# Key-value products three heads a matmul, a two-column tile of ones, and a last tile stored in three parts

## The chip, the cores and the metric

The kernel runs on one core of a Trainium2 chip. Its time is the device time of one execution in microseconds (us), and the median over several executions is quoted. The profile's span is about 1.4 us shorter than the time of the same execution. The three sets of experiments ran on three different chips, so each is compared in time with runs of the kernel before on its own chip; the kernel before has one profile only, from the start.

## The reference

Two linear-attention blocks A and B (sequence S = 2048, width D = 640, 32 heads of 20) read the same x; a sigmoid gate mixes their outputs. Shortened:

```python
def _A_ref(x, wqkv, wo):                      # _B_ref is the same
    q, k, v = split(x @ wqkv)                 # heads of 20
    phi = lambda t: jnp.where(t > 0, t + 1, jnp.exp(t)) + 1e-6
    pq, pk = phi(q), phi(k)
    kv  = einsum("bhsd,bhse->bhde", pk, v)    # 20 x 20 a head
    z   = einsum("bhsd->bhd", pk)
    num = einsum("bhqd,bhde->bhqe", pq, kv)
    den = einsum("bhqd,bhd->bhq", pq, z)[..., None] + 1e-6
    return (num / den).reshape(B, S, D) @ wo

g = sigmoid((x * gate_w).sum(-1, keepdims=True))
return g * a + (1 - g) * b
```

## The kernel before

The kernel first computes, for each branch, a Gram product of `pk` with x (lines L643 and L644, "Gram units" below), transposes it into `GS`, and multiplies that by the value weights `WV` to get the key-value products. This multiplication is the "burst" of L705. Six heads share a stationary tile of 128 columns, so a product holds blocks that belong to no head; the vector engine (DVE) multiplies by a 0/1 mask while it copies the product out of PSUM into `KVL`.

```python
KVL = {X: sb("KVL" + X, [128, NU, GR], bf) for X in XS}      # NU = 6, GR = 120
ONE = sb("ONE", [128, 128], bf)
...
for us in ((0, 1, 2, 3), (4, 5)):
    ps = Buf("kv", "ps")                    # one PSUM bank, from a pool of 8
    def fn(e, us=us, ps=ps):
        for i, u in enumerate(us):
            for c in range(NC):             # NC = 5
                lo, n, w = (GR * u, 128, 24) if u < 5 else (540, 104, 8)
                r = e.matmul(PS[0:n, ps.slot, GR * i : GR * i + NC * w],
                             WV[X][:, c, lo : lo + n], gv[:, c, :, 24 * u : 24 * u + w],
                             start=(c == 0), stop=(c == NC - 1))
    ...
    out(lambda ps=ps, n=n: PS[:, ps.slot, 0 : GR * n], us[0], n, 24, BDM, 0, 128)        # mask on DVE
    if 5 in us:
        out(lambda ps=ps: PS[64:104, ps.slot, GR : GR + 40], 5, 1, 8, BDE, 64, 104)
...
LAST = ((0, 512, "ACT"), (512, D, "DVE"))   # who copies which columns of the last output tile
def last_b(t):
    for (lo, hi, eng), ps in zip(LAST, blast):
        if hi == D:
            o_mm("A", t, ps, lo, hi)
        o_mm("B", t, ps, lo, hi)
        o_post(t, ps, lo, hi, eng, "ACT" if hi == D else "SP")   # copy, and store on this queue
```

A scheduler of the kernel's own puts the operations of each engine in order and gives out the PSUM banks when the program is built.

## Time and profile before

The median is 187.78 us (187.69 to 188.05, three runs); the profile has a span of 186.7 us. PE, the matrix engine, is the bound, so I cut the span where PE passes fixed points of the program. Each stage runs from the start of one matmul to that of another, in us:

| stage | before |
|---|---|
| start to first Gram matmul | 48.50 |
| first Gram matmul to first matmul of burst A | 52.07 |
| burst A to burst B | 41.63 |
| burst B to the last matmul | 42.15 |
| last matmul to the end of the span (the tail) | 2.32 |

The first stage contains the time at half clock, the last one the last copy and stores. "PE's stream" below is the sum of the three stages between them, 135.84 us here. The views print a span to 0.1 us; the tails in this document are taken to its unrounded end in the trace (186.669 us here). The expectations were written with rounded spans, so they name a tail of 2.36 us for 2.32. The prediction shows the engine totals, burst A and the tail. First, the timeline of PE after burst A and its query group: the Gram unit, whose first matmul starts at 103.18, and then the next query group. The first column is the start, the second how long the group is busy.

```profile
103.18 0.38 PE L643 MATMUL ps<-XN,PKB 128*128 128x512 bf16 x1
...
104.21 0.22 PE L644 MATMUL ps<-XN,PKB 128*128 128x129 bf16 x1
104.27 0.59 PE L797 MATMUL ps<-XT,WQB 128*128 128x512 bf16 x2
```

From 103.18 to 104.27 is 1.09 us, which is four pairs of 216 + 56 ns: PE doesn't wait. Second, the stores of the output by queue, with the shortest, median and longest duration in ns of the issuing instruction:

```profile
L354 SPq DMA_DIRECT2D out_dram<-TSB x16: 332/332/359, 164.8 to 184.7; - x16
L354 ACTq DMA_DIRECT2D out_dram<-TSB x1: 350/350/350, 185.0 to 185.0; - x1
```

Sixteen stores are issued on the queue of SP (an engine that issues transfers here), the last small one on that of the scalar engine (ACT), each in about a third of a microsecond.

### The profile page before, as it was taken

Reading aid. Unit: us, or ns where it says so; the run is one execution under the profiler, and the core shown is the slowest. Engines: PE = TensorE matmul, PEld = TensorE weight load, DVE = VectorE, ACT = ScalarE, POOL = GpSimd, SP = SyncE. Lnnn points to the kernel's source line nnn. Section 1 sums busy time; section 2 is a strip of 40 time slices with the busy share of each in tenths; the row PEclk is TensorE's granted clock in tenths of the full one; section 3 lists DMA queues with packets and bytes.
Section 4 is the critical chain, followed back from the end, with each engine's and each line's share of the span. In section 5 each row is a group of like instructions: output and inputs, shape, how many; then the busy total and the mean of one; then the engine's idle time right before and its main releaser. Section 6 shows DMA issues by size and latency. Waiting matters only on the chain.

```text
span 186.7 us, 3247 instructions
## 1 busy us (share of the span) xinstructions
PE 182.6 (98%) x1272; PEld 107.1 (57%) x1297; DVE 137.2 (73%) x264; ACT 95.0 (51%) x167; POOL 0.8 (0%) x10
## 2 busy tenths in 40 slices
PE   8999999999999999999999999999999999999995
PEld 4555555555555656555557555555567555555553
DVE  2289888888834455487799999998899999059563
ACT  5265655656454645544675666888623784400001
POOL 1000000000000000000000000000000000000000
PEclk9999999999999999999999999999999999999999
DMA  7989999995001011010511412126515447513424
GB/s 209 284 152 145 271 385 365 342 204 125 4 0 35 0 39 35 0 35 5 91 27 35 83 29 40 28 43 171 177 35 115 65 103 166 171 70 109 142 106 140
DMA packets 36501, 21.38 MB, mean 115 GB/s; under 512 B 25694, under 2 KB 36230, under 8 KB 36486
## 3 DMA queue, kind: packets, MB, share of 16 engines
q1 hardware_dynamic: 36044, 20.96, 44.7%
q10 hardware_dynamic: 442, 0.21, 0.4%
q8 instruction: 10, 0.16, 0.4%
q14 instruction: 5, 0.04, 0.1%
HBM read 10.87 MB, written 4.26 MB: 81 GB/s over the span
## 4 chain that ended last, share of the span: by engine, by line
PE 97%; DMA 1%; issue 1%; DVE 0%; DVEq 0%
PE ps L957 23%; PE ps L797 23%; PE ps L535 18%; PE ps L643 18%; PE ps L536 5%; PE ps L644 5%; PE ps L705 2%; DMA XN<-in_A_x_dram 1%; PE ps L740 1%; PE ps L479 1%; DVE TSB L1001 0%; PE ps L466 0%; DVEq L237 0%; PE ps L516 0%
## 5 line engine op out<-in xcount | busy, mean ns | idle before, releaser
L535 PE MATMUL ps<-WKW,XT 128*128 128x512 bf16 x154 | 43.8, 386 | 0.0
L814 ACT ACTIVATE EK<-ps 128x512 bf16<-128x512 f32 x40 | 23.9, 598 | 30.2 <-PE ps L797 27.9
L536 PE MATMUL ps<-WKW,XT 128*128 128x128 bf16 (+1 forms) x160 | 35.5, 222 | 0.3
L568 ACT ACTIVATE EK<-ps 128x640 bf16<-128x640 f32 x32 | 22.3, 704 | 10.7 <-DVE EK L571 5.3
L535 PEld LDWEIGHTS ps<-WKW,XT 128*128 128x128 bf16 x160 | 15.9, 99 | 19.1 <-issue 0.6
L797 PE MATMUL ps<-XT,WQA 128*128 128x512 bf16 x96 | 24.0, 379 | 0.1
L797 PE MATMUL ps<-XT,WQB 128*128 128x512 bf16 x96 | 23.6, 380 | 0.2
L643 PE MATMUL ps<-XN,PKA 128*128 128x512 bf16 x78 | 23.1, 379 | 0.1
L643 PE MATMUL ps<-XN,PKB 128*128 128x512 bf16 x78 | 23.1, 379 | 0.0
L824 DVE TENSOR_SCALAR EK<-EK 128x512 bf16<-128x512 bf16 x40 | 11.5, 289 | 13.5 <-ACT EK L814 13.5
L644 PE MATMUL ps<-XN,PKA 128*128 128x129 bf16 x80 | 17.6, 220 | 0.1
L644 PE MATMUL ps<-XN,PKB 128*128 128x129 bf16 x80 | 17.6, 220 | 0.1
L957 PE MATMUL ps<-WPA,EX 128*128 128x512 bf16 (+1 forms) x117 | 16.6, 297 | 0.2
L957 PE MATMUL ps<-WPB,PKA 128*128 128x512 bf16 (+1 forms) x118 | 16.4, 298 | 0.1
L536 PEld LDWEIGHTS ps<-WKW,XT 128*128 128x128 bf16 x160 | 15.9, 99 | 0.0
L797 PEld LDWEIGHTS ps<-XT,WQB 128*128 128x128 bf16 x100 | 10.9, 118 | 8.6 <-issue 0.4
L571 DVE TENSOR_SCALAR EK<-EK 128x640 bf16<-128x640 bf16 x32 | 10.4, 326 | 6.9 <-ACT EK L568 6.7
L797 PEld LDWEIGHTS ps<-XT,WQA 128*128 128x128 bf16 x100 | 10.7, 117 | 8.1
L643 PEld LDWEIGHTS ps<-XN,PKA 128*128 128x128 bf16 x80 | 9.4, 117 | 7.9
L643 PEld LDWEIGHTS ps<-XN,PKB 128*128 128x128 bf16 x80 | 9.4, 117 | 7.9
L579 DVE SCALAR_TENSOR_TENSOR PKA<-ps,EK 128x640 bf16<-128x640 f32 x16 | 13.2, 825 | 0.5
L579 DVE SCALAR_TENSOR_TENSOR PKB<-ps,EK 128x640 bf16<-128x640 f32 x16 | 13.2, 825 | 0.6
(77 smaller groups left out, 222.5 us busy)
## 6 DMA issues: line engine op xcount, KB each, us to landing
out_dram<-TSB SPq DMA_DIRECT2D x15, 160.0 KB, 1.8
XN<-in_A_x_dram SPq DMA_DIRECT2D x1, 2240.0 KB, 9.0
WKW<-in_A_wqkv_dram SPq DMA_DIRECT2D x5, 160.0 KB, 3.7
WKW<-in_B_wqkv_dram SPq DMA_DIRECT2D x5, 160.0 KB, 4.1
WQA<-in_A_wqkv_dram SPq DMA_DIRECT2D x1, 800.0 KB, 10.6
WQB<-in_B_wqkv_dram SPq DMA_DIRECT2D x1, 800.0 KB, 11.8
WVA<-in_A_wqkv_dram SPq DMA_DIRECT2D x1, 800.0 KB, 12.6
WVB<-in_B_wqkv_dram SPq DMA_DIRECT2D x1, 800.0 KB, 14.4
```

The lines of the kernel that those rows point to most:

```text
L535: e.matmul(a[:, 0:512], l, WK[X][:, c, 0:512], start=(c == 0), stop=(c == NC - 1))
L536: return e.matmul(a[:, 512:w], l, WK[X][:, c, 512:w], start=(c == 0), stop=(c == NC - 1))
L568: op("ACT", lambda e: e.activation(EK[:, ek.slot, :], psw(ps, D), ACT.Exp), act_cost(D), ins=[ps] + first, outs=[ek], name="ke")
L571: lambda e: e.tensor_scalar(EK[:, ek.slot, :], EK[:, ek.slot, :], 1.0, EPS, op0=ALU.min, op1=ALU.add),
L579: lambda e: e.scalar_tensor_tensor(PKt[X][:, t, :], psw(ps, D), 0.0, EK[:, ek.slot, :], op0=ALU.max, op1=ALU.add),
L643: e.matmul(a[:, 0:512], l, XN[:, t, 0:512], start=(t == 0), stop=(t == NT - 1))
L644: return e.matmul(a[:, 512 : D + 1], l, XN[:, t, 512 : D + 1], start=(t == 0), stop=(t == NT - 1))
L705: r = e.matmul(PS[0:n, ps.slot, GR * i : GR * i + NC * w], WV[X][:, c, lo : lo + n], gv[:, c, :, 24 * u : 24 * u + w], start=(c == 0), sto ...
L797: r = e.matmul(PS[:, ps.slot, :], WQ[X][:, c, g::5], XT[:, c, 512 * b : 512 * b + 512], start=(c == 0), stop=(c == NC - 1),)
L814: lambda e: e.activation(EQ[:, eq.slot, :], PS[:, ps.slot, :], ACT.Exp),
L824: lambda e: e.tensor_scalar(EQ[:, eq.slot, :], EQ[:, eq.slot, :], 1.0, EPS, op0=ALU.min, op1=ALU.add),
L957: r = e.matmul(a[:, l0 - lo : h0 - lo], PQ[X, b][:, g, 128 * (t % 4) : 128 * (t % 4) + 128], WP[X][:, g, l0:h0], start=(X == first and g = ...
```

## The change

No intent comes with it. What can be read off is that it saves SBUF, the memory beside the engines: 2 x 6 x 60 columns of `KVL`, 126 of `ONE` and 12 of the masks, 2 bytes each, are 1,716 bytes in each partition. Three things change, and they can be taken apart: the key-value part, the tile of ones, and the split end.

```diff
-    q, m = p % 64, np.arange(24)[None, :]
-    bd = np.where(p < 64, (q >= 4) & ((q - 4) // 20 == m // 4), (q < 60) & (3 + q // 20 == m // 4))
+    q, m = p % 64, np.arange(12)[None, :]
+    bd = np.where(p < 64, (q >= 4) & ((q - 4) // 20 == m // 4), (q < 60) & (q // 20 == m // 4))
...
-    KVL = {X: sb("KVL" + X, [128, NU, GR], bf) for X in XS}
+    KVL = {X: sb("KVL" + X, [128, NU, HR], bf) for X in XS}        # HR = 60
...
-    ONE = sb("ONE", [128, 128], bf)
+    ONE = sb("ONE", [128, 2], bf)              # its readers take ONE[:, 0:1] broadcast
...
-        for us in ((0, 1, 2, 3), (4, 5)):
+        for ts in (range(8), range(8, 11)):
...
-                        lo, n, w = (GR * u, 128, 24) if u < 5 else (540, 104, 8)
+                        lo, n, w = (GR * (t // 2), 128, 12) if t < 10 else (540, 104, 8)
                         r = e.matmul(
-                            PS[0:n, ps.slot, GR * i : GR * i + NC * w],
+                            PS[0:n, ps.slot, HR * i : HR * i + NC * w],
                             WV[X][:, c, lo : lo + n],
-                            gv[:, c, :, 24 * u : 24 * u + w],
+                            gv[:, c, :, 12 * t : 12 * t + w],
...
-            out(lambda ps=ps, n=n: PS[:, ps.slot, 0 : GR * n], us[0], n, 24, BDM, 0, 128)
+            for r in range(2):                 # upper and lower 64 partitions
+                out(lambda ps=ps, n=n, r=r: PS[64 * r : 64 * r + 64, ps.slot, 0 : GR * n]...[:, :, r, :],
+                    ts[0] // 2, n, 12, BDM[64 * r : 64 * r + 64, :], 64 * r, 64 * r + 64)
...
-    LAST = ((0, 512, "ACT"), (512, D, "DVE"))
+    LAST = ((0, 512, "ACT"), (512, 576, "DVE"), (576, D, "DVE"))
...
-            if hi == D:
+            if lo:
                 o_mm("A", t, ps, lo, hi)
             o_mm("B", t, ps, lo, hi)
-            o_post(t, ps, lo, hi, eng, "ACT" if hi == D else "SP")
+            o_post(t, ps, lo, hi, eng, "SP" if lo else "ACT")
```

## The prediction

> **What bounds the kernel now.** I read the page first, for the engine totals and the chain that ended last.
>
> ```profile
> PE 182.6 (98%) x1272; PEld 107.1 (57%) x1297; DVE 137.2 (73%) x264; ACT 95.0 (51%) x167; POOL 0.8 (0%) x10
> PE 97%; DMA 1%; issue 1%; DVE 0%; DVEq 0%
> ```
>
> The matrix engine PE is busy for 98% of the span of 186.7 us, and 97% of the chain of waits is PE itself. In the list of who waited for whom, PE's waits are 0.4 us for the tile of ones at the start and 0.2 us for the first input tile. Nothing holds it in the middle: where two matmul starts stand further apart than the matmul before them is wide, the excess is just one missing record (for instance 272 ns where 216 + 56 belong), apart from some 0.2 us at each of the four bursts that use 64-row tiles. So the time is a short head, one unbroken PE stream, and a tail after the last matmul. A change to the vector engine (DVE) or to buffers counts only if it makes PE wait.
>
> Next the timeline, for the stretches that the change touches. The first is the key-value burst of branch A on PE, then the weight loads (PEld) of the same line by form, then what DVE does with its result.
>
> ```profile
> 100.57 1.69 PE L705 MATMUL ps<-GSA,WVA 128*128 128x120 bf16 x30
> 102.11 0.81 PE L797 MATMUL ps<-XT,WQB 128*128 128x512 bf16 x3
> ...
> L705 PEld LDWEIGHTS ps<-GSA,WVA 128*128 128x128 bf16 x25 | 1.4, 98 | 0.2
> L705 PEld LDWEIGHTS ps<-GSA,WVA 128*104 128x104 bf16 x5 | 0.3, 128 | 0.0
> ...
> 101.90 2.13 DVE L685 TENSOR_TENSOR KVLA<-ps,CST 128x480 bf16<-128x480 f32 x3
> ```
>
> The burst costs PE 102.11 - 100.57 = 1.54 us from its first start to the next line's first start. The tail:
>
> ```profile
> 183.84 0.44 PE L957 MATMUL ps<-WPA,PKA 128*128 128x128 bf16 x5
> 184.10 0.60 ACT L1003 ACTIVATE TSB<-ps 128x512 bf16<-128x512 f32 x1 [21.89 <-PE ps L957]
> 184.12 0.44 PE L957 MATMUL ps<-WPB,GSA 128*128 128x128 bf16 x5
> 184.67 0.29 DVE L1001 CAST TSB<-ps 128x128 bf16<-128x128 f32 x1 [0.81 <-PE ps L957]
> 185.00 0.35 ACTq L354 DMA_DIRECT2D out_dram<-TSB  x1
> ```
>
> Ten matmuls of 128 columns, a copy of 0.29 us, an issue at 185.00 and a landing about 1.6 us after it (page, DMA issues) make the end at 186.7.
>
> **The price of one matmul in this trace.** Five matmuls of 128 columns take 184.12 - 183.84 = 0.28 us from start to start, 56 ns each. The chain has 30 matmuls of the output projection, 15 of 512 and 15 of 128 columns, in 4.08 us: 272 ns a pair, so 216 ns for 512 columns. The line through both is 0.417 ns a column plus 2.7 ns. It gives 52.7 ns at 120 columns; 25 of them are 1.32 us of the burst's 1.54, which leaves 0.22 us, 44 ns each, for the five matmuls of 40 columns, where the line would say 19 ns. Those five are the ones whose stationary tile has 104 columns: their loads last 128 ns and not 98. There the weight load, not the streaming, sets the pace.
>
> **What the Trainium skill says.** "TensorE: Matmul & The Clock Gate", section "Back-to-back issue gap", gives N/2.4 + 2.5 ns for a warm matmul; the line above agrees within 0.2 ns. The same section names a floor of about 25 ns for any N up to 64, and also about 62 ns a matmul where the sequencer decodes in software; the trace before has no long run of narrow matmuls, so it doesn't tell which floor this program has. The section "Weight-path perf modes — Fast Weight Load (FWL) and DoubleRow" says that a fast load is used when the stationary tile has 128 weights and isn't fp32; the 98 against 128 ns agree. "What's actually happening" in the same page puts the full clock after some 3.4 us of sustained activity; the trace has the full pace from 6.05 us, and PE busy without a gap from 2.7 us, which is 3.4 us earlier. "DMA: Bandwidth & Descriptors", section "Anatomy of one DMA — SWDGE (gpsimd) path", explains most of a DMA's fixed time as the write receipt; the three last stores here, of 160, 128 and 32 KB, land in 1.8, 1.7 and 1.6 us, so size hardly matters.
>
> **The change, part by part.** The build order of the changed kernel shows the same order on PE, with the burst split and the end split; ACT, POOL and SP keep theirs but for the last stores. DVE's order moves by a place here and there.
>
> (1) Key-value burst: per branch 25 matmuls of 120 columns become 50 of 60, and the five of 40 stay. The streamed columns are the same, 3,000; the fixed 2.7 ns and the weight load are paid twice. By the line 60 columns take 27.7 ns. The stationary tile keeps 128 columns, so the fast load should hide: five loads of 104 columns took 44 ns each, and a fast load must be well under that. Then a burst is 50 x 27.7 + 5 x 44 = 1.61 us against 1.54, +0.07 us, and +0.13 us for both branches. If a load and a matmul need some 30 ns together, it is 1.72 us, +0.36 us for both. I take +0.2 us. All of this is on the path, because PE never waits.
>
> (2) The masking on DVE: two operations of 64 partitions x 240 elements replace one of 128 x 480, and two of 64 x 60 one of 128 x 120. Elements along the free dimension are the same in sum, so the cost is two more instructions; DVE time goes by elements per partition, and the halves lie one after the other. The operation of 480 took 1.50 us and that of 40 took 0.275 us, which is 2.8 ns an element plus some 0.16 us. So 2 x 0.83 + 2 x 0.33 + 0.28 = 2.6 us against the 2.13 us in sequence: about +0.4 us per branch. None of it is on the path if it fits: for branch B the last masking ends at 145.57 us and PE's first user, the burst of L740, starts at 146.54, so about 0.9 us are spare. For branch A the user starts at 116.3, over 12 us later. DVE's later chain for branch B (scaling, first done at 154.9) has 7 us until PE needs it at about 162.
>
> (3) Ones as two columns: the fill on DVE took 0.17 us and will take perhaps 0.1 us less, so the first warming matmuls start at about 0.3 and not 0.39 us. They end before the first input tile lands at 2.6 us in either case, so nothing that counts moves. The full clock comes 3.4 us after PE's gapless activity starts at the landing of x, which is unchanged.
>
> (4) Last columns in two parts: 20 matmuls of 64 columns at 29.4 ns are 0.59 us against 10 x 56 = 0.56, +0.03 us. The last copy has 64 and not 128 columns, at about 1 ns a column -0.07 us. But both 64-column stores go to the SP queue, where an issue takes 0.33 us: first part copied at about 184.63, issued 184.66 to 184.99; second part copied at about 184.92 but issued at 184.99, when the queue is free. That is where the issue stood before, 185.00. Landing 1.6 us later: the gain is 0.0 to 0.05 us. The 512-column store moves to the ACT queue behind its own copy, at about 184.73, as before.
>
> Sum: +0.2 (1) + 0 (2) + 0 (3) + 0.0 (4) = +0.2 us, so 187.78 + 0.2 = 187.98; I say 187.95.
>
> **The rivals.** First: PE can't feed instructions fast enough. The burst becomes 110 instructions, a load and a matmul each 27.7 ns. For it speaks the software-decode figure above; against it that the L705 burst before ran 60 instructions at its streaming pace[...]. If it came, at 62 ns a matmul throughout, a burst would be 55 x 62 = 3.4 us, +1.9 us per branch and +3.7 us in all, 191.5 us, the one way to a loss of 2%. I give it 3%. Second: the masking of 64-partition operations costs more than its elements, say per row of the pattern, 1.5 us for each 240-element operation. It would be over 3 us, eat the 0.9 us of slack in branch B, and PE would wait some 0.5 us: 188.5 us. That the 40-element operation with short rows fits the price per element speaks against it. Third: the warm-up, started earlier, opens the full clock earlier. PE ran at half pace from 3.7 to 6.05 us; each us of that gone saves 0.5 us, so at most about -1 us, 187.0. The gap before the landing of x stays, which speaks against it. Fourth: the split tail gains its full 0.07 us or more; then the total is 187.9.
>
> **Range and chances.** Runs of the kernel before spread over 0.36 us. The sure terms run from +0.05 to +0.5 us; a drift between chips and a clock that opens slightly earlier pull below, a stretched burst above. I take 187.4 to 188.6. Within 2% means 184.0 to 191.5 us, and only the first rival reaches its edge; nothing I see reaches a gain of 3.8 us.
>
> **What would show each step.** For (1): the L705 burst of about 1.6 to 1.7 us from first start to the next line's, with matmul starts 27 to 30 ns apart; over 2 us says that the load or the feeding binds. For (2): the masking in about 2.6 us, and no wait of PE at the L740 burst of branch B. For (3): the first full-pace matmul at about 6.05 us still. For (4): two SP issues back to back, the second at about 185.0 plus what the burst added, and the last landing about 1.6 us after. I am wrong if PE shows a new wait, if the burst is over 2 us, or if the full clock comes at another time.

## The result, and the profile after

The changed kernel took 188.96 us (188.57 to 189.40, six runs) beside 187.98 us (187.69 to 188.58) of the kernel before in the same rounds. The ratio is 1.005, with a 95% interval of 1.0029 to 1.0071: slower by about 0.94 us, under the 2% that would be called slower, and outside the predicted range of 187.4 to 188.6. A ratio here is the mean time of one kernel's fast runs over that of the other's fast runs of the same rounds, so it isn't quite the ratio of the medians. All outputs are right.

The engine totals and the chain look as before:

```profile
PE 183.1 (97%) x1331; PEld 107.2 (57%) x1357; DVE 137.9 (73%) x269; ACT 95.0 (51%) x167; POOL 0.8 (0%) x10
PE 96%; DMA 1%; issue 1%; DVE 0%
```

PE is busy for 0.5 us more, the span is 1.3 us longer. The stages say where:

| stage | before | after | difference |
|---|---|---|---|
| start to first Gram matmul | 48.50 | 48.61 | +0.10 |
| first Gram matmul to burst A | 52.07 | 52.07 | 0.00 |
| burst A to burst B | 41.63 | 41.89 | +0.26 |
| burst B to the last matmul | 42.15 | 42.28 | +0.13 |
| tail | 2.32 | 3.15 | +0.83 |

The profile is of the slowest of the six runs, so its sum, 1.33 us, is more than the 0.94 us of the ratio. In the first stage the granted clock matters: full pace came at 6.35 us after the change and at 6.10 before, and a microsecond at half clock costs half a microsecond. Over all fourteen profiles, where the moment is recorded (eleven of them), it lies between 3.45 and 6.67 us and follows no part of the change. That is noise, and it is as large as the effect; the other stages are free of it.

**Burst A and what follows it.** The timeline, all engines, a few lines of it:

```profile
100.67 1.77 PE L705 MATMUL ps<-GSA,WVA 128*128 128x60 bf16 x55
...
102.05 2.50 DVE L685 TENSOR_TENSOR KVLA<-ps,CST 64x240 bf16<-64x240 f32 x5
102.25 0.81 PEld L805 LDWEIGHTS ps<-XT,WQB 128*128 128x128 bf16 x5
102.51 1.02 PE L805 MATMUL ps<-XT,WQB 128*128 128x512 bf16 x4
...
103.37 0.38 PE L643 MATMUL ps<-XN,PKB 128*128 128x512 bf16 x1
...
104.40 0.22 PE L644 MATMUL ps<-XN,PKB 128*128 128x129 bf16 x1
...
104.60 0.59 PEld L805 LDWEIGHTS ps<-XT,WQB 128*128 128x128 bf16 x4 [0.30 <-DVE KVLA L685]
104.61 0.84 PE L805 MATMUL ps<-XT,WQB 128*128 128x512 bf16 x3
```

The next line after the burst has five weight loads and four matmuls, so the record of its first matmul is missing; that one started a 512-column matmul (216 ns) before 102.51, at 102.29. The burst itself then takes 1.62 us from its first start to that of the next line, against 1.54, with starts 27.5 ns apart; in the four later kernels with the same burst and no record missing there it is 1.617 or 1.618 us. The Gram unit starts at 103.37, and the query group after it at 104.61: 1.24 us where it was 1.09. The bracket names the releaser: the masking, which runs to 102.05 + 2.50 = 104.55 and lets go of its PSUM bank then. PE needs that bank for the query group: the group reads nothing that the masking writes. Before, the masking was done at 101.90 + 2.13 = 104.03 and PE wanted the bank at 104.21, so the spare time was under 0.2 us. The wait is 0.15 us, and the second matmul of the group follows its first by 249 ns and not 216, which makes +0.18 us. With the burst's 0.08 that is the +0.26 of the stage.

**Branch B.** The masking is over before its reader is ready, as predicted: it ends at 143.87 + 2.50 = 146.37, and the reader (L748) starts at 146.99.

```profile
143.87 2.50 DVE L685 TENSOR_TENSOR KVLB<-ps,CST 64x240 bf16<-64x240 f32 x5
...
146.99 0.60 PE L748 MATMUL ps<-WOB,KVLB 64*60 64x320 bf16 x15
```

**The tail.** The same part of the timeline as the prediction shows of before; below it the stores by queue; below that the DMA queues (packets, megabytes, share) and issues (count, size, us from issue to landing), from 184 us on.

```profile
184.73 0.31 PE L965 MATMUL ps<-WPB,GSA 128*128 128x64 bf16 x5
185.18 0.35 ACTq L354 DMA_DIRECT2D out_dram<-TSB  x1
185.21 0.36 DVE L1009 CAST TSB<-ps 128x64 bf16<-128x64 f32 x2 [0.90 <-PE ps L965]
```

```profile
L354 SPq DMA_DIRECT2D out_dram<-TSB x17: 332/332/845, 165.2 to 185.8; - x17
```

```profile
q14 instruction: 1, 0.01, 0.9%
...
out_dram<-TSB ACTq DMA_DIRECT2D x1, 128.0 KB, 2.4
out_dram<-TSB SPq DMA_DIRECT2D x2, 16.0 KB, 2.2
```

Three things stand there that before did not have. The two 64-column copies belong to two products whose last groups of five matmuls began at 184.44 and at 184.73, 0.29 us apart, but the copies run as one block from 185.21, so the first was held until the second was ready too: it starts 0.36 us after the last matmul's start, and in three kernels below that have the same split it starts 0.01 us after it. Then the second store on the SP queue needed 845 ns to be issued, where 332 ns is usual. And a packet of 8 KB of "instruction" kind crossed on queue 14, at 185.90 us for 0.58 us. In the profile before there is none on that queue between 171.8 us and the end: the next one came at 187.93, 1.3 us after the span was over.

### The profile page after: what moved, and what is told of

Its sections match the earlier page's. It is cut to its first block, busy times and chain, and to the rows that moved or that the text cites. A ratio compares the mean times of both kernels' runs of the same rounds, so it can differ in the third digit from the quotient of the medians.

```text
span 188.0 us, 3374 instructions
## 1 busy us (share of the span) xinstructions
PE 183.1 (97%) x1331; PEld 107.2 (57%) x1357; DVE 137.9 (73%) x269; ACT 95.0 (51%) x167; POOL 0.8 (0%) x10
## 4 chain that ended last, share of the span: by engine, by line
PE 96%; DMA 1%; issue 1%; DVE 0%
PE ps L965 23%; PE ps L805 23%; PE ps L535 18%; PE ps L643 18%; PE ps L536 5%; PE ps L644 5%; PE ps L705 2%; DMA XN<-in_A_x_dram 1%; PE ps L748 1%; PE ps L479 1%; DVE TSB L1009 0%; PE ps L466 0%; PE ps L516 0%
## 6 DMA issues: line engine op xcount, KB each, us to landing
WVA<-in_A_wqkv_dram SPq DMA_DIRECT2D x1, 800.0 KB, 12.5
```

## The experiments

**First set: the parts alone.** Three kernels with one part each, and the changed kernel once more, five rounds each beside the kernel before (187.84 us, 187.21 to 188.51).

Key-value part alone: the changed kernel with these two undone.

```diff
-    ONE = sb("ONE", [128, 2], bf)
+    ONE = sb("ONE", [128, 128], bf)
-    LAST = ((0, 512, "ACT"), (512, 576, "DVE"), (576, D, "DVE"))
+    LAST = ((0, 512, "ACT"), (512, D, "DVE"))
```

> The kernel before with the key-value part alone (60-column matmuls, halved masking). Theory from the two profiles: each burst costs 0.08 us more (1.62 for 1.54 us) and branch A's masking holds a PSUM bank until 104.55, so that PE stands 0.18 us in the next query group: +0.34 us in all, the rest of the difference being elsewhere. Rival: the whole +1.0 us comes with this part (PE order or DVE order), then this run is at least 0.8 us slower than before. In the profile: a wait of PE for the masking of KVLA of about 0.2 us, none for KVLB.

Measured: 188.85 us, ratio 1.0062 (1.0036 to 1.0088). First Gram to last matmul is 136.22 us against 135.84 before: both bursts at +0.08 and the bank wait. But the tail is 3.50 us although its code is that of before, and its last copy starts 0.68 us after the last matmul instead of 0.33. DMA issues of its tail:

```profile
q14 instruction: 1, 0.01, 1.1%
...
out_dram<-TSB SPq DMA_DIRECT2D x1, 128.0 KB, 2.9
out_dram<-TSB ACTq DMA_DIRECT2D x1, 32.0 KB, 2.5
```

The same two stores took 1.7 and 1.6 us before. A store lands in 16 shares (16 updates of its semaphore in the trace; I take it for one on each of the 16 DMA engines, which the trace doesn't name): of the 128 KB one, 15 shares land by 2.05 us after the last matmul and the 16th at 3.27; of the 32 KB one 15 by 2.53 and the 16th at 3.45. One share of each store is late, not all.

Ones alone: the kernel before with `ONE` of two columns and its readers broadcast.

```diff
-    ONE = sb("ONE", [128, 128], bf)
+    ONE = sb("ONE", [128, 2], bf)
```

> The kernel before with the two-column tile of ones alone. Theory: the warming matmuls start 0.09 us earlier and still end before x lands, so nothing on the path moves: within 0.15 us of before, and the time at which the full clock comes scatters from run to run for both kernels. Rival: the full clock came 0.25 us later in the profile of the changed kernel because of this part; then the full clock comes at about 6.35 and not 6.1 us here too, and the time is +0.1 us.

Measured: 187.58 us, ratio 0.9989 (0.9961 to 1.0016): nothing in the total. The tail is 2.32 us, as before. There is a small wait for the bank even here (the list of waits: waiter, releaser, us in total, times, longest), because the masking ended 1.12 us after the Gram unit's start and not 0.85:

```profile
PEld ps L797 <- DVE KVLA L685: 0.2, 1, 0.2
```

So the spare time at that bank is a matter of what DVE happens to do ahead of the masking.

Split end alone:

```diff
-    LAST = ((0, 512, "ACT"), (512, D, "DVE"))
+    LAST = ((0, 512, "ACT"), (512, 576, "DVE"), (576, D, "DVE"))
-            if hi == D:
+            if lo:
-            o_post(t, ps, lo, hi, eng, "ACT" if hi == D else "SP")
+            o_post(t, ps, lo, hi, eng, "SP" if lo else "ACT")
```

> The kernel before with the last 128 columns in two parts alone. Theory: this part has the most of the loss; PE ends 0.05 us later, the first copy waits, the two stores go one after the other through the SP queue, and the second issue takes 0.85 us for 0.33 because an instruction fetch falls beside it: +0.5 to +0.9 us. Rival: the fetch and the long issue came from the instructions of all parts together and are absent here; then it is within 0.4 us of before, with the second issue at 0.33 us.

Measured: 188.74 us, ratio 1.0051 (1.0023 to 1.0079). Both copies are on time (0.01 and 0.23 us after the last matmul), and the SP issue takes 0.43 us and not 0.85. The tail is 3.08 us all the same: 15 of 16 shares of the last store land by 2.32 us, the 16th at 3.04, and an instruction packet was under way at +1.69 us. Its profile has the shortest head of all, because the full clock came at 3.45 us:

```profile
3.56 0.38 PE L535 MATMUL ps<-WKW,XT 128*128 128x512 bf16 x1
3.77 0.22 PE L536 MATMUL ps<-WKW,XT 128*128 128x128 bf16 x1
```

Five hundred and twelve columns from 3.56 to 3.77 are the full pace. This span is 186.4 us, shorter than that of the kernel before, while the median is 0.9 us longer. Whoever compares spans alone gets the sign wrong here.

The changed kernel again:

> The changed kernel again, on the same chip as its parts: +1.0 us as measured. If the parts add, it is the sum of the three runs beside it within 0.2 us. Its profile should again have the instruction fetch beside the second of the two last stores, and an issue of about 0.85 us.

Measured: 188.71 us, ratio 1.0041 (1.0019 to 1.0063), and the same picture in the trace: bank wait, copies at 0.36 and 0.50 us, an SP issue of 0.76 us, the packet at +1.05, a tail of 3.07 us.

What follows: by the medians the key-value part alone costs 1.0 us, the split end alone 0.9, and both together no more than either. Costs that don't add point to a common cause. What the two parts share is that they make the program of DVE longer: 316 recorded instructions (its waits for semaphores included) before, 320 with the key-value part, 318 with the split end, 322 with both, and 316 with the ones alone. And in each of the slow ones an instruction packet falls into the tail. The Trainium skill, "Runtime: NRT & Kernel Launch", section "Instruction fetch mechanics", says that an engine's instructions are fetched in blocks by a DMA queue while the engine runs, at a cost that is mostly hidden. My theory from here: the DVE program crosses a block end near its 320th recorded instruction; the crossing holds the engine for a third of a microsecond, and the fetch that follows delays what shares its DMA engine. Normally that is hidden, but not in the last three microseconds. The rival: the tail suffers from what the parts themselves do there, the split copies and the two stores on one queue.

**Second set: the same program, longer or shorter.** Beside the kernel before (187.97 us, 187.28 to 188.76).

Four idle fills ahead in the kernel before, 320 instructions on DVE, nothing else:

```diff
+    PAD = sb("PAD", [128, 4], f32)
     op("DVE", lambda e: e.memset(ONE[:, :], 1.0), 120.0, outs=[bone], name="one")
+    for i in range(4):
+        op("DVE", lambda e, i=i: e.memset(PAD[:, i : i + 1], 0.0), 60.0, name="pad")
```

> The kernel before with four one-column fills more on DVE at the start, where DVE is idle, and nothing else: 320 DVE instructions for 316. Theory (instruction fetch): the 320th traced DVE instruction starts about 0.35 us late and brings an 8 KB instruction fetch about 1 us later, which holds up one DMA engine; here the 320th is the last copy of the kernel. So the tail from the start of the last matmul to the end is 2.9 to 3.5 us for 2.36, and the time +0.6 to +1.1 us, with PE's order unchanged. Rival: the tail depends on the split stores or on the key-value part; then nothing happens here, the tail stays at 2.36 us and the time within 0.2 us.

Measured: 188.69 us, ratio 1.0033 (1.0016 to 1.0051), PE's stream 135.84 us as before, tail 3.21 us for 2.32. Timeline and DMA issues of the tail:

```profile
184.07 0.44 PE L960 MATMUL ps<-WPB,GSA 128*128 128x128 bf16 x5
184.97 0.29 DVE L1004 CAST TSB<-ps 128x128 bf16<-128x128 f32 x1 [1.16 <-PE ps L960]
185.29 0.36 ACTq L355 DMA_DIRECT2D out_dram<-TSB  x1
```

```profile
q14 instruction: 1, 0.01, 1.1%
...
out_dram<-TSB SPq DMA_DIRECT2D x1, 128.0 KB, 2.6
out_dram<-TSB ACTq DMA_DIRECT2D x1, 32.0 KB, 2.2
```

The copy starts 0.90 us after its five matmuls began, in the kernel before 0.55 us (184.67 - 184.12). Four fills of one column each in the first microseconds put 0.9 us onto the tail and 0.6 us onto the time. The view names PE as releaser because that was the last semaphore; but DVE's instruction that waits for PE was over at 184.57, and the copy followed 0.396 us later, where 0.044 us is usual.

Twenty-four fills in the kernel before (the same edit with 24):

> The same with 24 fills. Theory (instruction fetch): the 320th DVE instruction is now some 20 places before the end, about at 172 us, so stall and fetch fall among the output adds, where DVE has spare time; the tail is 2.36 us again and the time that of before within 0.3 us, although this kernel does more than the one with four fills. Rival: more DVE instructions cost time in themselves, then it is slower than the run with four.

Measured: 187.67 us, ratio 0.9982 (0.9961 to 1.0003), tail 2.33 us. Twenty more instructions than the last kernel, and the loss is gone. DVE's 320th instruction is now one at 171.05 us. It follows the wait ahead of it by 0.415 us, where the same instruction follows by 0.20 us in three kernels below in which it isn't the 320th, and PE doesn't wait for it. This kernel also speaks for whose fetch it is: an earlier packet, which came at DVE's 191st instruction in the kernel before (111.09 us), comes again at the 191st, but at 101.00 us, though PE, ACT and SP run as before.

Twenty-four fills in the changed kernel:

> The changed kernel with the 24 fills at the start. Theory (instruction fetch): the tail falls from 3.1 to at most 2.4 us, and what is left of the loss against before is the two bursts, the bank wait and the longer end on PE, +0.4 us (0.16 + 0.18 + 0.05) for +0.9. Rival: the two stores one after the other on one queue make the tail long; then it stays at 3.0 us or more and the time at +0.9 us.

Measured: 188.00 us, ratio 0.9994 (0.9974 to 1.0014), tail 2.31 us. Its timeline, and its stores by queue:

```profile
184.25 0.31 PE L968 MATMUL ps<-WPB,GSA 128*128 128x64 bf16 x5
184.37 0.45 DVE L1012 CAST TSB<-ps 128x64 bf16<-128x64 f32 x2 [0.55 <-PE ps L968]
```

```profile
L355 SPq DMA_DIRECT2D out_dram<-TSB x17: 332/332/430, 164.8 to 185.0; - x17
```

The split copies run when their products are complete, and the longest SP issue is 0.43 us. The rival falls: the same split end, with the same two stores on one queue, ends in 2.31 us, as the unsplit one in 2.32. PE's stream is still 136.25 us, with its wait for the bank.

Key-value products with 64 stationary columns: three heads are in 64 columns, so the upper and lower half of a unit can be separate matmuls into separate halves of PE, with half of the columns each and no wasted block. The masking then is three operations again and DVE's program 316.

```diff
-                        r = e.matmul(
-                            PS[0:n, ps.slot, HR * i : HR * i + NC * w],
-                            WV[X][:, c, lo : lo + n],
-                            gv[:, c, :, 12 * t : 12 * t + w], ...)
+                        for h in (0, 64) if u < 5 else (64,):
+                            n, w = (64, 12) if u < 5 else (40, 8)
+                            r = e.matmul(
+                                PS[h : h + n, ps.slot, HR * i : HR * i + NC * w],
+                                WV[X][:, c, (GR * u + h if u < 5 else 604) : ... + n],
+                                gv[:, c, :, 24 * u + (12 * h // 64 if u < 5 else 0) : ... + w], ...)
```

> The kernel before with the idea of the change taken further: each 60-column matmul over only the 64 stationary columns that it needs, the two halves of a unit alternating into the two partition halves of one bank, and one masking operation of 128 partitions for both. DVE has 316 instructions as before. Theory: the two halves run side by side on PE, so a burst takes about 0.8 us for 1.54 and the masking 1.5 us for 2.13; no PE wait for a bank, tail 2.36: -1.4 us. Rival: loads of 64 columns lose the fast load and the matmuls go one after the other, 30 ns each: the burst stays at 1.6 us and the time at that of before.

Measured: 186.93 us, ratio 0.9943 (0.9922 to 0.9964): faster than both kernels, 1.0 us below the one before, clear of noise though under the 2%.

```profile
100.32 1.10 PE L706 MATMUL ps<-GSA,WVA 128*64 128x60 bf16 x55
101.26 1.32 DVE L685 TENSOR_TENSOR KVLA<-ps,CST 128x240 bf16<-128x240 f32 x3 [0.42 <-PE ps L706]
101.35 0.80 PEld L797 LDWEIGHTS ps<-XT,WQB 128*128 128x128 bf16 x5
```

The two matmuls of a pair start 3 ns apart and a pair takes 31.6 ns, so the burst is 1.03 us to the next line's start, and the masking 1.32 us. PE's stream is 135.07 us, 0.77 less. I had expected 1.4 us less in the time. Part of the miss lies at the change of tile size: the burst's first matmul starts 309 ns after the wide one ahead of it where 216 are usual, and the next wide one 112 ns after the burst's last where 25 are usual, about 0.09 us each, 0.36 us for two bursts. The Trainium skill, "TensorEngine Tiling (Array Packing)", section "Key Properties", says that a change of tiling mode drains the engine; these gaps agree, though no run here isolates the drain, and the page has no number. The rest of the miss is the burst itself, of which I had expected 0.8 us.

**Third set: each part with the fetch moved away, and the bank wait by itself.** Beside the kernel before (188.09 us, 187.70 to 188.19).

The key-value part with 24 fills, and the split end with 24 fills (the edits shown above, together):

> The key-value part alone with the 24 fills on DVE, which move the instruction fetch away from the end. Theory: what is left is PE's own cost, 0.16 us for the two bursts and 0.15 to 0.18 us for the bank wait: from the first matmul of the key Gram products to the last matmul of the kernel +0.35 us against before (135.84 us there), tail 2.3 to 2.4 us, time +0.35 us against the kernel before and at least 0.5 us under the same part without fills. Rival: the key-value part costs 1.1 us in itself; then the fills change nothing.

> The split end alone with the 24 fills. Theory: PE ends 0.05 us later, the second store is issued 0.64 us after the last matmul starts, as the 128-column one was (0.65), and lands 1.65 us later: tail 2.3 to 2.4 us, time within 0.2 us of before, neither gain nor loss. Rival: the split costs by its second store on the same queue: tail 2.7 us or more.

Measured: 188.03 us, ratio 1.0004 (0.9991 to 1.0017), tail 2.31 us, for the key-value part, and 187.81 us, ratio 1.0012 (0.9978 to 1.0047), tail 2.33 us, for the split end. Each part alone had lost 0.9 to 1.0 us; without the fetch in the tail neither shows a loss in the total. In PE's stream the split end costs 0.06 us (135.90), the key-value part 0.49 us (136.33), of which 0.29 is the wait for the bank:

```profile
PEld ps L808 <- DVE KVLA L688: 0.4, 1, 0.4
```

A longer masking in the kernel before with 24 fills: the mask of the second bank is applied once more, into a scratch tile. It needs no other matmuls.

```diff
+    KVX = {X: sb("KVX" + X, [128, 1, GR], bf) for X in XS}
...
+            if 5 in us:
+                out(lambda ps=ps, n=n: PS[:, ps.slot, 0 : GR * n], 0, n, 24, BDM, 0, 128, KVX[X])
```

> The kernel before with 24 fills and one masking operation of 120 elements done twice in each branch (the copy goes to a tile that nobody reads). No matmul changes. Theory (bank): PE's next query group after the burst of branch A starts 0.06 us after the last masking ends; the masking ends 0.6 us later than before, so PE stands about 0.4 us there, and from the first Gram matmul to the last matmul it takes 136.25 us for 135.84; nothing is lost in branch B. Rival: the 0.15 us gap beside the changed kernel's masking has another cause (a lost record, a slower load); then PE's time here stays at 135.84 us.

Measured: 188.36 us, ratio 1.0028 (0.9995 to 1.0060), PE's stream 136.03 us, tail 2.33 us. The wait appears with nothing else of the change present:

```profile
PEld ps L803 <- DVE KVLA L689: 0.3, 1, 0.3
```

It is 0.15 us, where I had expected 0.4: the masking ended only 0.32 us later than in the kernel with 24 fills alone, counted from the Gram unit's start. In the total, five of the six runs average 0.2 us over the kernel before; the sixth, at 190.13 us, lifts the mean to the 0.5 us of the ratio. All seven profiles in which PE waits there follow one sum: the wait is the end of the masking, counted from the Gram unit's start, plus 0.057 us, less the unit's 1.090. It gives 0.147 and 0.157 us for the changed kernel's two profiles, 0.172 and 0.288 for the key-value part without and with fills, 0.156 for the changed kernel with fills, 0.085 for the ones alone and 0.148 here; the traces show the same to a few ns.

Two fills in the kernel before:

> The kernel before with two fills: 318 DVE instructions, as the split end alone had. Theory (instruction fetch): the last copy is the 318th and starts on time (0.33 us after the last matmul starts), but the fetch comes about 1.7 us after that start, between the last stores, as in the split end alone, and holds one of 16 landings back by 0 to 0.8 us: tail 2.4 to 3.1 us. Rival: the late landing of the split end alone came from its small stores; then the tail here is 2.3 to 2.4 us with no fetch before the end.

Measured: 188.01 us, ratio 1.0001 (0.9988 to 1.0013), tail 2.33 us. The packet is in the tail, at +1.80 us, and does no harm; I had expected a tail of 2.4 to 3.1 us:

```profile
q14 instruction: 1, 0.01, 1.3%
...
out_dram<-TSB SPq DMA_DIRECT2D x1, 128.0 KB, 1.7
out_dram<-TSB ACTq DMA_DIRECT2D x1, 32.0 KB, 1.6
```

So a packet in the tail is not enough; with 318 instructions the held one lies beyond the last copy, and by my theory the packet must also meet a share of a store on its DMA engine. In the split end alone, with 318 too, a share was late; that the two met on one engine isn't shown.

All fourteen together, ordered by the length of DVE's program. Times are counted from the last matmul's start. A packet some 12.5 us ahead of it is in every kernel; where DVE's program is longest it is the last one. The nine kernels without a packet in the tail, or with two fills, end in 2.31 to 2.33 us, the other five in 3.07 to 3.50:

| kernel | DVE instructions | last packet on queue 14 | tail, us |
|---|---|---|---|
| before | 316 | +3.59 | 2.32 |
| ones alone | 316 | +3.59 | 2.32 |
| 64 columns | 316 | +3.77 | 2.31 |
| before, 2 fills | 318 | +1.80 | 2.33 |
| split end alone | 318 | +1.69 | 3.08 |
| before, 4 fills | 320 | +1.35 | 3.21 |
| key-value alone | 320 | +1.37 | 3.50 |
| changed kernel | 322 | +1.06 | 3.15 |
| changed, again | 322 | +1.05 | 3.07 |
| before, 24 fills | 340 | -12.5 | 2.33 |
| split end, 24 fills | 342 | -12.6 | 2.33 |
| long masking, 24 fills | 342 | -12.6 | 2.33 |
| key-value, 24 fills | 344 | -12.3 | 2.31 |
| changed, 24 fills | 346 | -12.6 | 2.31 |

## Why the prediction was wrong

The steps that failed are (4), by which the end gains 0.0 to 0.05 us (the tail measured +0.83), and (2), by which nothing of the masking is on the path (PE waited 0.15 us for it in branch A). The direction of the PE terms was right; the total was missed because of these two terms, which the sum didn't contain.

**(1) Burst: right.** I took +0.2 us for both branches, with 1.61 to 1.72 us a burst. It is 1.62 us, starts 27.5 ns apart (27.7 predicted), +0.16 us. The first rival, that PE can't be fed, is refuted: 50 matmuls in a row at 27.5 ns, each with its load.

**(2) "None of it is on the path if it fits": wrong for branch A.** The size was near (2.50 us for 2.6), and so was branch B. The price per element held for the new operations (0.83 to 0.85 us for 240 elements, 0.32 to 0.34 for 60, of 0.83 and 0.33), though the 40-element one, being an end of the line, couldn't test it, and the old one of 120 took 0.59 us where the line gives 0.50. That the +0.4 us came out near +0.37 is partly luck: 2.6 is a sum of single durations, set against 2.13 us in sequence, in which operations overlap (their own sum is 2.36), and 2.6 - 2.13 is 0.47. For branch A I looked only at who reads `KVL`, 12 us later. But the masking also holds a PSUM bank, and that is let go when the masking ends. The next owner of the bank was a query group that needed it less than 0.2 us after the old end. The masking ended 0.52 us later in the trace. Of this, 0.10 us is the later head and 0.08 us the longer burst, which move PE as well; 0.19 us is the spare time; 0.15 us is left. Cost: 0.15 us of waiting and 0.03 us for the matmul after it. The long masking shows this with the change absent. The second rival named the right waiter for the wrong reason: the masking's price was as predicted, and PE waited for it all the same, at a place where I hadn't looked.

**(3) Ones: right that it doesn't count** (ratio 0.9989). Wrong in its reason: I took the 3.4 us between PE's first gapless work and the full clock as a rule, from one trace in which it fitted. Over the runs the full clock comes anywhere from 3.45 to 6.67 us, for kernels whose heads are alike, which is 0.96 to 4.02 us after the first matmul that reads x. The first Gram matmul then starts anywhere from 47.41 to 48.84 us, which moves single runs by more than the whole effect. The third rival, an earlier full clock from the earlier warm-up, isn't seen: the ones alone had it at 5.82 us, inside that scatter. One profile a kernel can't exclude it, but the times don't show it either.

**(4) "The gain is 0.0 to 0.05 us": wrong by 0.8 us in the profile.** PE's part is +0.05 us for the predicted +0.03. The working of the queues was right as such: with the fetch out of the way the second store of the split end is issued 0.64 us after the last matmul, for 0.65 of the one store before. But the split end's tail is then 2.31 to 2.33 us, as without the split, and PE ends 0.06 us later, so it gives no gain at all (and the fourth rival's 0.07 us is not reached). The section that I cited for the landing is about transfers issued from gpsimd; these are issued by SP and ACT, and no run here splits their 1.6 us. What no step and no rival held is that the change adds six instructions to DVE's program, and that the 320th of that program can be an expensive one. In the kernel before the program ends four short of it. The changed kernel makes it the first of the two last copies, which then waits for 0.35 us; the second store is issued at +0.99 us and not at +0.65; its issue takes 0.85 us and not 0.35; it lands 1.28 us after the issue is over, as before (15 of its shares by 2.92 us, the last at 3.11). The sum is 0.99 + 0.85 + 1.28 = 3.12 us, against 0.65 + 0.35 + 1.28 = 2.28: 0.84 us, where the tails differ by 0.83.

That the length of DVE's program is the cause is shown by the times: four fills in an unchanged kernel cost 0.6 us, 24 fills cost nothing, and the changed kernel with 24 fills is level with the kernel before (0.9994).

What stays open: How the length acts is inferred. The records don't name the engine that a fetch serves; that it is DVE's is inferred from its moving with DVE's count and from the gap in DVE. The hold is not a rule for every such packet: of the nine kernels with 320 or more DVE instructions six show it at the 320th, each time right behind an instruction that waits for a semaphore, and three don't (the long masking and the two padded ones with the key-value part, where the one ahead of the 320th is not a wait). Around the 191st DVE never stands idle for more than 0.11 us, in any of the fourteen. That the long SP issue comes from the fetch is inferred from the two coming together, in both profiles of the changed kernel and in none of the others. Why the fetch did harm with 318 instructions in the split end and none with two fills isn't known. The totals of the padded kernels differ from what their stages add up to by up to 0.5 us, in either direction: the changed one with fills has 0.41 us more on PE and the same time, the long masking 0.19 us more on PE and 0.5 us in the total, most of that from one run. The key-value part with fills has 0.49 us more on PE, and the interval of its time ends at +0.32 us. The scatter of the head is large enough for that, but I have not shown that it is the cause, so the bank wait is shown in the stages and not in a total. In the two padded kernels with the key-value part a packet came at about 150.3 us, at DVE's 303rd instruction, which I can't explain; their last one near the end, at -12.6 and -12.3 us, is at DVE's 324th, and one is there in the kernel before too.

## What to carry to other kernels

Count the instructions of each engine that a change adds, and look at what the last few microseconds hold: here a handful of instructions at the start of DVE's program put 0.9 us onto the last stores, by what looks like the end of a fetch block with its stall and its transfer, and twenty idle ones more took it out again. When an operation that empties PSUM gets longer, ask who takes its bank next, not only who reads what it writes. Where the total scatters by more than the effect, cut the span at fixed points of the program and compare stages, and undo parts one by one: parts that don't add up point to a cause they share.

## What the Trainium skill lacked or had wrong

- "Runtime: NRT & Kernel Launch", section "Instruction fetch mechanics", gives blocks of 16 KiB, 256 instructions, and a cost that is mostly hidden. The runs show packets of 8 KB (8,192 bytes) that I take for DVE's, mostly near the 191st and the 320th recorded instruction, 129 apart; by the page's size of an instruction 8 KB are 128 of them (an estimate). In two kernels the later packet comes at the 303rd. Packets of the page's 16 KB are there too, ten of them on queue 8. Where DVE is held at the 320th, that follows the wait ahead of it by 0.395 to 0.415 us, where 0.044 us is usual in the tail and 0.20 at 171 us. In the tail the loss is 0.75 to 1.2 us (tails of 3.07 to 3.50 us against 2.32).
- No page that I read says that such a fetch can delay a store. With a packet in the tail one of 16 shares of one or two of the stores landed 0.55 to 1.2 us after the other 15, in all five kernels with a long tail; with two fills none was late. That packet and share use the same DMA engine isn't shown.
- "TensorE: Matmul & The Clock Gate", section "Back-to-back issue gap": its formula fits down to 60 columns (27.5 ns). Its sustained 81 ns at 128 and 131 ns at 512 columns are not seen (56 and 216 ns, with a load each), and neither is the 62 ns of software decoding.
- The same page, section "What's actually happening", puts the scatter of the full clock at 500 ns either way; the runs show 3.45 to 6.67 us, of which up to 0.5 us can be the landing of the first input (first matmul on x at 2.28 to 2.80 us).
- "TensorEngine Tiling (Array Packing)", section "Key Properties", has no figure for the drain between tile sizes: gaps about 0.09 us longer on each side of a burst here. Pairs of 64-column matmuls started 3 ns apart, 31.6 ns a pair.
